# Three-pass gate chunk, tap sums on TensorE, a new order of work and warm-up matmuls in a convolution and two feed-forward layers

## The chip, the cores and the metric

The kernel runs on one core of one Trainium2 chip. The metric is the device time of one execution, in microseconds (us). Its parts are TensorE (PE, with PEld for its weight loads), VectorE (DVE), ScalarE (ACT), GpSimd (POOL) and SyncE (SP), which here only issues DMAs.

## The reference

Batch 2, sequence 4160, model width 192, 8 heads, 7 taps, inner width 1024, all in float32 for the reader (the weights come to the chip as 64-bit words and are narrowed there).

```python
def _attn_ref(x, weight_gen):          # 7-tap dynamic convolution
    w = softmax over the 7 taps of weight_gen      # (B, S, 8, 7)
    return einsum('bshk,bskhg->bshg', w, windows of 7 rows of x)

def _moe_ref(x, mu_k, mu_r, w_k, w_v, w_r):
    xk = mu_k * x + (1.0 - mu_k) * x_prev          # x_prev: x shifted by one row
    xr = mu_r * x + (1.0 - mu_r) * x_prev
    k = np.maximum(xk @ w_k, 0.0)                  # 192 -> 1024
    v = k * k @ w_v                                # 1024 -> 192
    r = 1.0 / (1.0 + np.exp(-(xr @ w_r)))          # the gate, 192 -> 192
    return r * v

def _moe2_ref(x, w_in, conv_w, w_out):
    h = np.maximum(x @ w_in, 0.0)                  # 192 -> 1024
    conv_out = 3-tap convolution of h along the sequence, by column
    return h * sigmoid(conv_out) @ w_out           # 1024 -> 192
```

The output is `_moe2_ref(_moe_ref(_attn_ref(x)))`.

## The kernel before, in words

**Tiles.** The sequence is cut into ten tiles (`SIZES`: 238, 238, seven of 476, 352), each with two batches. The inner width is cut into eight chunks of 128 (`fi` or `j`). A value in float32 is kept as a high and a low part in a matmul type of fewer bits, so that one product of two such values takes three matmul passes.

**Attention** (`attention`, 530). For each slot of a tile `token` (538) makes the seven products of rows and softmax weights in one instruction over 1344 elements (`prod`), then sums them over the taps. For tile 0 the products are made on DVE and the sum is seven matmuls with the identity on PE (`total`). For every later tile POOL makes the product and three adds. Two `rows` buffers and two `prod` buffers go round.

**Mixing** (`mixing`, 574). The sums are transposed on PE, mixed with the row before (`mu`, `onemu`) and split: `xA` holds model columns 0 to 127 (high and low), `xB` packs the last 64 columns, high part on one half of the lanes and low part on the other; SP copies these halves from `rm` and a scratch buffer.

**First layer.** `gate_r` (664) makes the gate for 128 output columns, `k=0`, and for the other 64, `k=1`; the columns of `k=1` are kept twice, so both halves of the lanes hold them. `passes_in` (660) is five passes: two weights parts by the high part of `xA`, one by the low part, two by `xB`. `moe1` (682) makes the chunk, relu, square, split (`s`), and `out_passes` (797) five passes into the banks `am` and `ar`. `mix_out` (818) multiplies by the gate and writes `X = x2[b]`: rows 0 and 1 high and low of columns 0 to 127, rows 2 and 3 the last 64.

**Second layer.** `moe2` (854) makes a chunk in bank `pc` (five passes), relu, three taps, sigmoid, product, the high part `g` by ACT (`c7`) and the low part by DVE, or by POOL from tile 7 on (`c8`); `out_passes` into `bm` and `br`; `store` (913) sends it out.

**Weights.** Sixteen chunks are fetched in the first part of the run (`prepare`, 478). `narrow` (399) turns a chunk of 64-bit words into float32 with ACT, DVE and two PE matmuls (identity and `signs`), and `split` (423) takes high and low part with one more PE matmul of `signs`.

**Order.** Nothing is issued directly. Every piece of work is put on a plan with `at(t, ...)` at a due time; the table `ORDER` shifts single entries of that plan by number (368). `Program.schedule` then walks through all recorded operations with a cost for each (`cost`), takes for each engine the ready operation that is due first, and replays the result engine by engine. That is why nearly all instructions carry line 237 in the profile (650 in the changed kernel). SP works its DMAs off in that order, one after the other: an entry whose semaphores are not there holds back all behind it.

Of the kernel before, what the change touches and what calls it, by code (L numbers as in the profile page):

```python
# [96 lines left out]
class Program:
# [986 lines left out]
```

## Time and profile before

| | |
|---|---|
| runs of the kernel | 734.06, 736.1, 736.75 us; median 736.1 |
| profiled execution, its own time | 739.15 us |
| profiled execution, span | 737.3 us |
| instructions | 10455 |
| PE busy | 706.5 us (96%), 3475 instructions |
| ACT / DVE / POOL busy | 646.6 (88%) / 580.1 (79%) / 537.8 us (73%) |
| mean granted TensorE clock | 0.989 of full speed |
| chain that ended last | PE 80%, POOL 8%, ACT 6%, issue 3%, DVE 2%, DMA 1% |

The span reaches from the first to the last instruction; the profiled execution's own time is 1.85 us more, and lies 3.05 us above the median. A PE record lasts longer than the pace at which PE goes on, since matmuls overlap at their ends: starts of successive records show the pace.

### The profile page before, as it was taken

The page shows a single profiled execution, that of the slowest core. Times are in us where ns is not written, and L with a number is a line of the kernel's source. Part 1 is how long each engine was busy: PE and PEld are TensorE (multiplying, and loading weights), DVE is VectorE, ACT ScalarE, POOL GpSimd, SP SyncE. Part 2 cuts the span into 40 slices and gives each one's busy share as a digit, 9 for nine tenths or more (in the row PEclk, how much of TensorE's full clock was granted, in tenths as well). Part 3 has the DMA queues.
Part 4 walks back from the last instruction along what each step waited for, and adds up shares of the span by engine and source line. Part 5 has one row for each costly group of instructions (what it writes and reads, how often), then busy time and mean ns, then how long its engine had stood idle before and what let it go on. Part 6 is the DMA issues. An engine that isn't in the chain of part 4 may idle for free.

```text
span 737.3 us, 10455 instructions
## 1 busy us (share of the span) xinstructions
PE 706.5 (96%) x3475; PEld 607.1 (82%) x3475; DVE 580.1 (79%) x959; ACT 646.6 (88%) x1340; POOL 537.8 (73%) x392
## 2 busy tenths in 40 slices
PE   4899988999999999999999999999999999999996
PEld 4687966888778888888888888888888888899995
DVE  5865968887998988787878787978796758686775
ACT  2788859999989999899989898989899989899986
POOL 1998997898999899999999999999022323242333
PEclk9899999999999999999999999999999999999999
DMA  8667112101211320231112202210002000200000
GB/s 271 196 198 228 56 54 54 39 35 59 68 39 55 88 75 1 73 80 48 54 58 57 87 1 69 74 48 1 21 15 59 1 20 7 55 0 21 1 21 29
DMA packets 18149, 44.58 MB, mean 60 GB/s; under 512 B 2864, under 2 KB 13616, under 8 KB 17968
## 3 DMA queue, kind: packets, MB, share of 16 engines
q1 hardware_dynamic: 18096, 43.93, 19.7%
q8 instruction: 27, 0.44, 0.3%
q14 instruction: 26, 0.21, 0.1%
HBM read 27.40 MB, written 6.39 MB: 46 GB/s over the span
## 4 chain that ended last, share of the span: by engine, by line
PE 80%; POOL 8%; ACT 6%; issue 3%; DVE 2%; DMA 1%; POOLq 0%; SPq 0%; ACTq 0%; DVEq 0%
PE pa L237 25%; PE pc L237 18%; PE bm L237 12%; PE am L237 11%; PE br L237 8%; PE ar L237 7%; POOL prod L237 5%; ACT pa L237 1%; DMA mu<-in_mu_dram 1%; ACT pc L237 1%; POOL s L237 1%; ACT L237 1%; DVE stage L237 1%; POOL xA L237 1%; POOL tok L237 0%
## 5 line engine op out<-in xcount | busy, mean ns | idle before, releaser
L237 DVE SCALAR_TENSOR_TENSOR pc<-h,cw,pc 128x476 f32<-128x476 f32 (+1 forms) x276 | 194.3, 705 | 40.4 <-ACT pc L237 37.4
L237 POOL TENSOR_TENSOR prod<-rows,sw 128x1344 f32<-128x1344 f32 x68 | 210.4, 3096 | 16.1 <-PE pa L237 15.2
L237 ACT ACTIVATE pa<-pa 128x476 f32<-128x476 f32 (+2 forms) x284 | 153.1, 540 | 31.7 <-PE pa L237 28.5
L237 POOL TENSOR_TENSOR prod<-prod 128x576 f32<-128x576 f32 (+1 forms) x132 | 161.5, 1223 | 9.3
L237 PE MATMUL bm<-g,wo 128*128 128x476 f32 (+1 forms) x411 | 133.1, 378 | 3.3 <-ACT g L237 2.8
L237 PE MATMUL am<-s,wv 128*128 128x476 f32 (+2 forms) x464 | 135.1, 359 | 0.0
L237 PE MATMUL pa<-xA,wkA 128*128 128x476 f32 (+2 forms) x450 | 117.6, 366 | 2.0 <-DVE s L237 1.5
L237 POOL TENSOR_TENSOR g<-stage,g 128x476 fp32r<-128x476 f32 (+1 forms) x41 | 47.5, 1158 | 97.5 <-ACT g L237 93.6
L237 PE MATMUL pc<-x,wiA 128*128 128x478 f32 (+1 forms) x414 | 113.2, 379 | 0.7 <-ACT x L237 0.6
L237 PE MATMUL ar<-s,wv 128*128 128x476 f32 (+2 forms) x336 | 106.5, 355 | 3.6 <-ACT s L237 3.6
L237 DVE TENSOR_TENSOR s<-pa,s 128x476 fp32r<-128x476 f32 (+1 forms) x139 | 88.1, 634 | 18.7 <-ACT s L237 18.2
L237 PE MATMUL br<-g,wo 128*128 128x476 f32 (+1 forms) x274 | 102.5, 375 | 0.0
L237 PEld LDWEIGHTS pa<-xA,wkA 128*128 128x128 f32 x450 | 79.7, 189 | 19.1 <-DVE s L237 5.5
L237 ACT ACTIVATE pc<-h,cw 128x476 f32<-128x476 f32 (+1 forms) x138 | 92.4, 670 | 1.2
L237 PEld LDWEIGHTS am<-s,wv 128*128 128x128 f32 x464 | 82.1, 189 | 11.2 <-ACT s L237 0.9
L237 DVE TENSOR_TENSOR pc<-h,pc 128x476 f32<-128x476 f32 x96 | 62.8, 654 | 33.7 <-ACT pc L237 33.5
L237 PEld LDWEIGHTS bm<-g,wo 128*128 128x128 f32 x411 | 75.9, 188 | 15.4 <-ACT g L237 4.3
L237 ACT ACTIVATE pc<-pc 128x476 f32<-128x476 f32 (+1 forms) x148 | 81.2, 548 | 8.2 <-DVE pc L237 6.5
L237 PEld LDWEIGHTS pc<-x,wiA 128*128 128x128 f32 x414 | 76.2, 190 | 12.7 <-DVE g L237 2.0
L237 ACT ACTIVATE h<-pc 128x478 f32<-128x478 f32 (+1 forms) x138 | 79.0, 573 | 8.4 <-PE pc L237 7.5
L237 PE MATMUL pa<-xB,wkB 128*128 128x476 f32 (+2 forms) x300 | 84.5, 361 | 0.6 <-DMA xB<-mk 0.6
L237 PE MATMUL pc<-x,wiB 128*128 128x478 f32 (+1 forms) x276 | 82.4, 377 | 0.0
(161 smaller groups left out, 1190.0 us busy)
## 6 DMA issues: line engine op xcount, KB each, us to landing
rows<-in_x_dram SPq DMA_DIRECT2D x14, 960.0 KB, 4.8
xB<-rm SPq DMA_DIRECT2D x28, 119.0 KB, 2.3
rows<-in_x_dram SPq DMA_DIRECT2D x4, 768.0 KB, 6.5
xB<-mk SPq DMA_DIRECT2D x16, 119.0 KB, 2.3
rows<-in_x_dram SPq DMA_DIRECT2D x2, 864.0 KB, 4.3
out_dram<-stage SPq DMA_DIRECT2D x7, 238.0 KB, 2.0
out_dram<-om SPq DMA_DIRECT2D x7, 238.0 KB, 2.0
stage<-in_moe_w_v_dram SPq DMA_DIRECT2D x4, 384.0 KB, 6.0
```

The source lines that it names most:

```text
L237: getattr(self.real[eng], method)(*a, **k)
```

## The change

- `gate_r`, `k=1`: the weights of the 64 columns are now stored as [high | low] side by side in 128 columns (`swap`, two DMAs), so that three passes give high and low products at once; `fold` copies the upper 64 lanes down with ACT and adds them with DVE, the sigmoid runs on 64 lanes, and a DMA copies the result to the other 64 lanes. This holds for tiles 2 to 9.
- `mix_out`: the ACT copy of 64 lanes into `X[0:64, 3]` becomes a DMA from `X[0:64, 2]`.
- `SUMS`: six slots of tiles 1 and 2 have their taps summed by seven matmuls on PE and an ACT copy, not by POOL.
- `MODES`: seven of the sixteen weight chunks are narrowed and split without PE, with two more DVE operations.
- `softmax`: for the later tiles the addition of 1e-9 goes from DVE to ACT (seven instructions).
- Last tile, last batch: the high part of chunks 0 to 4 goes from ACT to POOL (`HIGH`), the low part of chunks 6 and 7 from POOL to DVE (`LOWS`), and the last `out_passes` ends `ar`'s bank ahead of `am`'s (`back`).
- `WARM`: 18 matmuls of `signs` over 256 columns into the idle bank `ar`, ahead of PE's first instruction.
- `mu` comes with the first softmax load; its own DMA is gone. The last softmax load is due later (20.5, hold 60).
- The table `ORDER` is replaced as a whole.

The diff, without the table and without the layout on the host:

```diff
+WARM = 18
+HIGH = range(5)
+LOWS = {(NTILE - 1, NB - 1, k) for k in range(6, NF)}
+SUMS = {(1, 1, 0), (1, 1, 1), (2, 0, 2), (2, 0, 3), (2, 1, 2), (2, 1, 3)}
+MODES = [0, 0, 0, 0, 0, 0, 0, 0, 2, 2, 2, 0, 2, 2, 2, 2, 2]
...
         if method == "dma_start":
-            return 0.45, 0.0
+            return 0.58 if src == ["SBUF"] else 0.45, 0.0
...
             eng, method, a, k = self.ops[i][:4]
+            if eng == "PE" and self.warm:
+                self.warm = self.warm()
             getattr(self.real[eng], method)(*a, **k)
...
         def s5():
-            DVE.tensor_scalar(z, z, 1e-9, None, op0=ALU.add)
+            if bank is None:
+                ACT.activation(z, z, ACTF.Copy, bias=1e-9)
+            else:
+                DVE.tensor_scalar(z, z, 1e-9, None, op0=ALU.add)
             DVE.reciprocal(m, z)
...
     def split(dst_hi, dst_lo, x):
+        if isinstance(x, Parts):
+            px, zl, zr = x.aps
+            ACT.copy(dst_hi, px)
...
+                DVE.tensor_tensor(zl, px, f(dst_hi), op=ALU.subtract)
+                DVE.tensor_tensor(dst_lo, zr, f(zl), op=ALU.add)
+            return
...
-            if i < 1:
+            if i < 1 or (i, b, l) in SUMS:
...
                     for k in range(KS):
                         PE.matmul(z, lhsT=ident, rhs=y[:, k], start=(k == 0), stop=(k == KS - 1))
                     x = tok_t[i][:, :, b * DM:b * DM + DM]
+                    if i:
+                        ACT.copy(x[:, l], z)
+                        return
...
-            sl = slice(128 * k, 128 * k + 128)
-            mm(p[:, :N], passes_in(wrA, wrB, xin[i, b, 1, 0], xin[i, b, 1, 1], sl, N))
+            A, B = xin[i, b, 1, 0], xin[i, b, 1, 1]
+            if k:
+                mm(p[:, :N], [(wrA[:, 0, 128:256], A[:, 0, :N]), (wrA[:, 0, 128:256], A[:, 1, :N]), (wrB[:, 0, 128:256], B[:, :N])])
+            else:
+                mm(p[:, :N], passes_in(wrA, wrB, A, B, slice(0, 128), N))
+
+        def fold():
+            a = attt_r()[0:64, :N]
+            ACT.copy(a, st["p"][64:128, :N])
+            DVE.tensor_tensor(st["p"][0:64, :N], st["p"][0:64, :N], a, op=ALU.add)
 
         def sg():
             r = r_r[k]()
             r_t[k] = r
-            ACT.activation(r[:, :N], st["p"][:, :N], ACTF.Sigmoid)
-
+            ACT.activation(r[h, :N], st["p"][h, :N], ACTF.Sigmoid)
+            if k:
+                SP.dma_start(out=r[64:128, :N], in_=r[0:64, :N])
...
         def a1():
-            ACT.copy(X[0:64, 3, c], r[0:64, :N])
             ACT.copy(X[:, 2, c], r[:, :N])
+            SP.dma_start(out=f(X[0:64, 3, c]), in_=f(X[0:64, 2, c]))
...
-            ACT.copy(g[:, 0, :N], st["q"][:, :N])
+            if (i, b) == (NTILE - 1, NB - 1) and fi in HIGH:
+                POOL.tensor_copy(g[:, 0, :N], st["q"][:, :N])
+            else:
+                ACT.copy(g[:, 0, :N], st["q"][:, :N])
 
         def c8():
             g = st["g"]
-            (POOL if i >= ALONE else DVE).tensor_tensor(g[:, 1, :N], st["q"][:, :N], f(g[:, 0, :N]), op=ALU.subtract)
+            (POOL if i >= ALONE and (i, b, fi) not in LOWS else DVE).tensor_tensor(g[:, 1, :N], st["q"][:, :N], f(g[:, 0, :N]), op=ALU.subtract)
...
     def consts():
-        SP.dma_start(out=mu, in_=mus)
...
+    def swap():
+        for W in (wrA, wrB):
+            SP.dma_start(out=f(W[:, 0, DM:256]), in_=f(W[:, 1, 128:DM]))
+
+    at(30.5, swap)
...
+    def warm():
+        for _ in range(WARM):
+            nc.tensor.matmul(ar_r.tiles[0][:, 0:256], lhsT=signs[:, 0:128], rhs=signs[:, 0:256], start=True, stop=True)
+
+    prog.warm = warm
```

**Where the order moves.** In the rows below a name with a number is one buffer; what is in brackets are the semaphores an instruction waits for (of an engine, or of a DMA queue).

The first place is POOL's start, the tokens of tile 1 (`rows1` holds one batch, `rows0` the other). Before:

```order
L237 TENSOR_TENSOR prod1_84<-rows1_82,sw_112 128x1344 [waits DMAHW0_49,DMAHW6_49,DVE_49,PE_49]
L237 TENSOR_TENSOR prod0_83<-rows1_82,sw_112 128x1344 [waits PE_49]
L237 TENSOR_TENSOR prod1_84<-rows0_81,sw_112 128x1344 [waits DMAHW2_49,DVE_49,DMAHW7_49,PE_49,Pool_49]
L237 TENSOR_TENSOR prod0_83<-rows0_81,sw_112 128x1344 [waits PE_49,Pool_49]
L237 TENSOR_TENSOR prod0_83<-prod0_83 128x576 [waits Pool_49]
```

and in the changed kernel:

```order
L650 TENSOR_TENSOR prod0_82<-rows1_81,sw_111 128x1344 [waits DMAHW0_49,DMAHW6_49,DVE_49,PE_49]
L650 TENSOR_TENSOR prod1_83<-rows1_81,sw_111 128x1344 [waits DVE_49,PE_49]
L650 TENSOR_TENSOR prod0_82<-rows0_80,sw_111 128x1344 [waits DMAHW1_49,DVE_49,DMAHW5_49,PE_49,Pool_49]
L650 TENSOR_TENSOR prod0_82<-prod0_82 128x576 [waits Pool_49]
L650 TENSOR_TENSOR prod0_82<-prod0_82 128x384 [waits Pool_49]
```

POOL's first product now goes into the buffer of the first tap sum, `prod0`, where before it went into that of the second, `prod1`; and two products for PE's sums stand ahead of the first adds in both.

The second place is PE at the tap sums and transposes of tile 2, among the first layer of tile 1 and the second of the first unit. Before:

```order
L237 MATMUL pa1_114<-ident_64,tok0_85 128x128 [waits Pool_49]
L237 MATMUL pa1_114<-ident_64,tok0_85 128x128 x3
L237 MATMUL ar_118<-s0_105,wv_70 128x238 [waits Activation_49]
L237 MATMUL ar_118<-s0_105,wv_70 128x238 x2
L237 MATMUL ar_118<-s0_105,wv_70 128x238 [waits DVE_49]
L237 MATMUL ar_118<-s0_105,wv_70 128x238 x6
```

and in the changed kernel:

```order
L650 MATMUL pa1_113<-prod0_82,ident_63 128x192 [waits Pool_49]
L650 MATMUL pa1_113<-prod0_82,ident_63 128x192 x6
L650 MATMUL ar_117<-s1_105,wv_69 128x238 [waits DVE_49]
L650 MATMUL ar_117<-s1_105,wv_69 128x238 x5
L650 MATMUL pa1_113<-ident_63,tok0_84 128x128 [waits Activation_49]
L650 MATMUL pa1_113<-ident_63,tok0_84 128x128
L650 MATMUL pc1_115<-prod1_83,ident_63 128x192 [waits Pool_49]
L650 MATMUL pc1_115<-prod1_83,ident_63 128x192 x6
L650 MATMUL pa1_113<-ident_63,tok0_84 128x128 x2
L650 MATMUL pa0_112<-ident_63,tok0_84 128x128
```

The transposes (`tok0`) waited for POOL's last add; now they wait for ACT's copy of a sum that PE itself made from POOL's product.

The third place is SP's queue at the load of rows for the next tiles. Before:

```order
L237 DMA rows0_81<-in_x_dram 128x1920 [waits DMAHW7_49,Pool_49]
L237 DMA rows1_82<-in_x_dram 128x1920 [waits DMAHW0_49,Pool_49]
L237 DMA out_0_dram<-stage_76 128x476 [waits DMAHW1_49,Activation_49]
L237 DMA out_0_dram<-att0_87 64x476 [waits DMAHW2_49,DVE_49]
L237 DMA xB01_98<-rm00_91 64x476 [waits DMAHW3_49,PE_49,Activation_49]
```

and in the changed kernel:

```order
L650 DMA rows0_80<-in_x_dram 128x1920 [waits DMAHW7_49,Pool_49]
L650 DMA x2_1_74<-x2_1_74 64x476 [waits DMAHW0_49,PE_49,Activation_49]
L650 DMA rows1_81<-in_x_dram 128x1920 [waits DMAHW1_49,Pool_49]
L650 DMA r10_103<-r10_103 64x476 [waits DMAHW2_49,DVE_49,Activation_49]
L650 DMA out_0_dram<-stage_75 128x476 [waits DMAHW3_49,Activation_49]
L650 DMA out_0_dram<-stage_75 64x476 [waits DMAHW4_49,DVE_49]
L650 DMA x2_0_73<-x2_0_73 64x476 [waits DMAHW5_49,PE_49,Activation_49]
```

The copies of the gate (`r10`) and of `X` (`x2_1`, `x2_0`) stand in the same queue, some of them behind a load of rows that waits for POOL to leave its buffer.

## Rows read from the trace of the kernel before

**Rows 1.** Busy time of the engines in five stretches of the run.

```profile
core 0: us, PE busy (x) PEld busy (x) DVE busy (x) ACT busy (x) POOL busy (x), PEclk, DMA share, GB/s
0.00:20.00 20.00, 9.51 (x38) 8.09 (x38) 11.42 (x22) 5.84 (x15) 4.21 (x9) 1.00 0.79 259
20.00:85.00 65.00, 60.49 (x389) 51.41 (x390) 49.60 (x96) 54.51 (x143) 59.89 (x43) 0.95 0.61 189
85.00:125.00 40.00, 32.28 (x163) 26.42 (x163) 29.33 (x46) 28.87 (x56) 33.95 (x25) 0.91 0.18 50
...
250.00:500.00 250.00, 249.93 (x1168) 213.91 (x1167) 204.70 (x329) 228.02 (x456) 241.03 (x164) 1.00 0.19 57
720.00:737.30 17.30, 11.16 (x55) 8.57 (x55) 9.38 (x19) 10.65 (x25) 6.58 (x7) 0.92 0.10 31
```

**Rows 2.** The same view, two stretches of 2 us after tile 1.

```profile
92.00:94.00 2.00, 0.73 (x7) 0.53 (x5) 1.28 (x2) 2.00 (x5) 1.96 (x2) 1.00 0.00 0
98.00:100.00 2.00, 2.00 (x9) 1.80 (x8) 0.66 (x1) 0.81 (x3) 1.92 (x3) 0.55 0.00 0
```

**Rows 3.** Chain that ended last: start us, us, what; the same place of two tiles.

```profile
351.71 1.51 PE pa L237 x9
...
427.08 1.53 PE pa L237 x9
```

**Rows 4.** Timeline of PE at a gate chunk: start us, us, engine, line, operation.

```profile
215.77 0.60 PE L237 MATMUL pa<-xA,wrA 128*128 128x476 f32 x2
216.20 0.59 PE L237 MATMUL pa<-xB,wrB 128*128 128x476 f32 x2
```

**Rows 5.** Timeline of PE at tap sums: the first two, and a later one.

```profile
10.22 6.88 PE L237 MATMUL pa<-prod,ident 128*128 128x192 f32 x28 [10.22 <-DVE prod L237]
...
23.14 2.44 PE L237 MATMUL pa<-prod,ident 128*128 128x192 f32 x14
```

**Rows 6.** Timeline of PE at weight chunks: identity pairs and a `signs` matmul.

```profile
22.91 0.40 PE L237 MATMUL br<-wkA,signs 128*128 128x512 f32 x1
...
66.16 1.02 PE L237 MATMUL bm<-stage,ident 128*128 128x512 f32 x2
...
74.40 0.81 PE L237 MATMUL bm<-stage,ident 128*128 128x384 f32 x2
```

**Rows 7.** Timeline of POOL: first product, adds and next product, last add of tile 2.

```profile
16.54 6.04 POOL L237 TENSOR_TENSOR prod<-rows,sw 128x1344 f32<-128x1344 f32 x2 [15.19 <-PE pa L237]
...
83.12 2.53 POOL L237 TENSOR_TENSOR prod<-prod 128x576 f32<-128x576 f32 x2
...
86.28 3.08 POOL L237 TENSOR_TENSOR prod<-rows,sw 128x1344 f32<-128x1344 f32 x1
...
104.60 0.59 POOL L237 TENSOR_TENSOR tok<-prod 128x192 f32<-128x192 f32 x1
```

**Rows 8.** Timeline of ACT and of DVE in the first 10 us.

```profile
2.23 0.30 ACT L237 ACTIVATE signs<-ident 128x128 fp32r<-128x128 f32 x1
...
8.43 0.17 DVE L237 TENSOR_SCALAR onemu<-mu 128x4 f32<-128x4 f32 x1 [2.58 <-DMA mu<-in_mu_dram]
```

**Rows 9.** Timeline of POOL, DVE and PE, 215 to 220 us.

```profile
215.07 3.08 POOL L237 TENSOR_TENSOR prod<-rows,sw 128x1344 f32<-128x1344 f32 x1
...
216.14 2.06 DVE L237 TENSOR_SCALAR stage<-stage 128x48 f32<-128x48 f32 x1
...
219.43 0.93 PE L237 MATMUL pa<-xA,wkA 128*128 128x476 f32 x3 [1.35 <-DVE s L237]
```

**Rows 10.** Timeline of DVE at `mix_out`, an operation over 64 lanes.

```profile
202.58 0.65 DVE L237 TENSOR_TENSOR x<-ar,x 64x476 fp32r<-64x476 f32 x1
```

**Rows 11.** Timeline of POOL in the tail: the last low part.

```profile
731.31 0.94 POOL L237 TENSOR_TENSOR s<-stage,s 128x354 fp32r<-128x354 f32 x1 [0.67 <-ACT s L237]
```

**Rows 12.** Page, DMA issues: queue, count, KB each, us from issue to landing.

```profile
xB<-rm SPq DMA_DIRECT2D x28, 119.0 KB, 2.3
```

**Rows 13.** Waits of SP: waited for, us in total, times, longest us.

```profile
SPq L237 <- POOL prod L237: 199.4, 16, 27.2
```

More of the change, by code (lines that the diff above doesn't have):

```diff
@@ L103, in __init__ @@
         self.real = {"PE": nc.tensor, "ACT": nc.scalar, "DVE": nc.vector, "POOL": nc.gpsimd, "SP": nc.sync}
+    warm = None
     def engine(self, name):
@@ L251, in conv_moe_kernel @@
 @with_exitstack
-def conv_moe_kernel(ctx: ExitStack, tc: tile.TileContext, xp, wg_first, wg_rest, mus, w_k, w_v, w_r, w_in, conv_w, w_out, out):
+def conv_moe_kernel(ctx: ExitStack, tc: tile.TileContext, xp, wg_first, wg_rest, w_k, w_v, w_r, w_in, conv_w, w_out, out):
     nc = tc.nc
@@ L285, in __call__ @@
             return self.tiles[(self.n - 1) % len(self.tiles)]
-    mu = new("mu", [128, 4])
     onemu = new("onemu", [128, 4])
@@ L311, in conv_moe_kernel @@
     wz_r = Ring([t.rearrange("p a b -> p (a b)") for t in g_r.tiles[:2]])
+    wl_r = Ring([t.rearrange("p a b -> p (a b)") for t in g_r.tiles[2:]])
     rows_r = ring("rows", 2, [128, max(SLOTS) + PAD, DM])
@@ L328, in conv_moe_kernel @@
     KH = KS * NH
-    sw = new("sw", [128, sum(slots), KS, NH])
+    both = new("sw", [128, 4 + sum(slots) * KH])
+    mu = both[:, 0:4]
+    sw = both[:, 4:].rearrange("p (s k h) -> p s k h", k=KS, h=NH)
     sm = []
@@ L395, in fetch, with __init__, rearrange, __getitem__ @@
         return st
-    on_pe = [False]
+    mode = [0]
+    class Parts:
+        def __init__(self, *aps):
+            self.aps = aps
+        def rearrange(self, *a, **k):
+            return Parts(*(x.rearrange(*a, **k) for x in self.aps))
+        def __getitem__(self, c):
+            return Parts(*(x[c] for x in self.aps))
     def narrow(st, n):
@@ L404, in narrow @@
         x, y, z = px.bitcast(U32), py.bitcast(U32), wy_r()[:, :n]
-        if on_pe[0]:
+        ACT.activation(px, f(hi), ACTF.Prelu, scale=2.0 ** -112, alpha=-(2.0 ** 32))
+        if mode[0] == 0:
             zr = wz_r()[:, :n]
-            ACT.activation(px, f(hi), ACTF.Prelu, scale=2.0 ** -112, alpha=-(2.0 ** 32))
             DVE.tensor_scalar(z, x, 3, None, op0=ALU.logical_shift_left)
@@ L414, in narrow @@
             return px
-        ACT.activation(px, f(hi), ACTF.Copy, scale=2.0 ** -112)
         DVE.tensor_scalar(x, x, 3, None, op0=ALU.logical_shift_left)
-        DVE.scalar_tensor_tensor(out=x, in0=hi, scalar=0x80000000, in1=x, op0=ALU.bitwise_and, op1=ALU.bitwise_or)
         DVE.tensor_scalar(y, x, 0xFF800000, None, op0=ALU.bitwise_and)
-        DVE.scalar_tensor_tensor(out=f(z), in0=lo, scalar=2.0 ** -52, in1=py, op0=ALU.mult, op1=ALU.mult)
-        DVE.tensor_tensor(px, px, f(z), op=ALU.add)
-        return px
+        zr = wz_r()[:, :n] if mode[0] == 1 else py
+        DVE.scalar_tensor_tensor(out=zr, in0=lo, scalar=2.0 ** -52, in1=py, op0=ALU.mult, op1=ALU.mult)
+        return Parts(px, wl_r()[:, :n], zr)
     def split(dst_hi, dst_lo, x):
+        if isinstance(x, Parts):
+            px, zl, zr = x.aps
+            ACT.copy(dst_hi, px)
+            if mode[0] == 1:
+                DVE.tensor_tensor(zl, px, f(dst_hi), op=ALU.subtract)
+                PE.matmul(px, lhsT=signs[:, 0:128], rhs=zl, start=True, stop=False, skip_group_check=True)
+                PE.matmul(px, lhsT=signs[:, 0:128], rhs=zr, start=False, stop=True, skip_group_check=True)
+                ACT.copy(dst_lo, px)
+            else:
+                DVE.tensor_tensor(zl, px, f(dst_hi), op=ALU.subtract)
+                DVE.tensor_tensor(dst_lo, zr, f(zl), op=ALU.add)
+            return
         ACT.copy(dst_hi, x)
-        if on_pe[0] and prog.space(x) == "PSUM":
+        if prog.space(x) == "PSUM":
             PE.matmul(x, lhsT=signs[:, 128:256], rhs=dst_hi, start=False, stop=True, skip_group_check=True)
@@ L486, in use @@
             def use(st=st, n=n, go=go, j=j):
-                on_pe[0] = j < 16
+                mode[0] = MODES[j]
                 go(narrow(st[0], n))
@@ L495, in softmax_load @@
     def softmax_load(j, wg, t, hold=0.0):
-        w = sm[j][0]
-        at(t, lambda: SP.dma_start(out=w.rearrange("p s k h -> p (s k h)"), in_=wg), hold)
+        w = both[:, (4 + KH * soft_at[j]) * (j > 0):4 + KH * soft_at[j + 1]]
+        at(t, lambda: SP.dma_start(out=w, in_=wg), hold)
     def softmax(j, a, b, eng, times, bank):
@@ L676, in sg @@
             r_t[k] = r
-            ACT.activation(r[:, :N], st["p"][:, :N], ACTF.Sigmoid)
+            ACT.activation(r[h, :N], st["p"][h, :N], ACTF.Sigmoid)
+            if k:
+                SP.dma_start(out=r[64:128, :N], in_=r[0:64, :N])
+        h = slice(0, 64 if k else 128)
         at(t, go)
-        at(t + 0.3, sg)
+        if k:
+            at(t + 0.2, fold)
+        at(t + (0.6 if k else 0.3), sg)
     def moe1(i, b, fi, t):
@@ L795, in mix_out_half, with out_passes @@
         at(t + 0.4, d2)
-    def out_passes(W, fi, s, n, am, ar, one=False):
+    def out_passes(W, fi, s, n, am, ar, one=False, back=False):
         s0, s1 = s[:, 0, :n], s[:, 1, :n]
@@ L802, in out_passes @@
         PE.matmul(ar[:, :n], lhsT=W[:, fi, 2], rhs=s0, start=a and not one, stop=False, skip_group_check=one)
-        PE.matmul(am[:, :n], lhsT=W[:, fi, 0], rhs=s1, start=False, stop=z, skip_group_check=one)
-        PE.matmul(ar[:, :n], lhsT=W[:, fi, 2], rhs=s1, start=False, stop=z, skip_group_check=one)
+        for p, k in ((ar, 2), (am, 0)) if back else ((am, 0), (ar, 2)):
+            PE.matmul(p[:, :n], lhsT=W[:, fi, k], rhs=s1, start=False, stop=z, skip_group_check=one)
     def carry(i, b, t):
@@ L889, in c7 @@
             st["g"] = g
-            ACT.copy(g[:, 0, :N], st["q"][:, :N])
+            if (i, b) == (NTILE - 1, NB - 1) and fi in HIGH:
+                POOL.tensor_copy(g[:, 0, :N], st["q"][:, :N])
+            else:
+                ACT.copy(g[:, 0, :N], st["q"][:, :N])
         def c8():
             g = st["g"]
-            (POOL if i >= ALONE else DVE).tensor_tensor(g[:, 1, :N], st["q"][:, :N], f(g[:, 0, :N]), op=ALU.subtract)
+            (POOL if i >= ALONE and (i, b, fi) not in LOWS else DVE).tensor_tensor(g[:, 1, :N], st["q"][:, :N], f(g[:, 0, :N]), op=ALU.subtract)
         def go2():
@@ L899, in go2 @@
                 acc2["r"] = br_r()
-            out_passes(wo, fi, st["g"], N, acc2["m"], acc2["r"])
+            out_passes(wo, fi, st["g"], N, acc2["m"], acc2["r"], back=last and b == NB - 1 and fi == NF - 1)
         at(t + 0.5, go)
@@ L971, in conv_moe_kernel @@
     softmax(2, 0, slots[2], DVE, (0.9, 0.91, 0.92, 0.93, 0.94, 0.95), am_r.tiles[0])
-    softmax_load(3, wg_rest[:, (slots[1] + slots[2]) * KH:], 18.2, 50.0)
+    softmax_load(3, wg_rest[:, (slots[1] + slots[2]) * KH:], 20.5, 60.0)
     for j in range(NTILE - 3):
@@ L1018, in conv_moe_kernel @@
         fn()
+    def warm():
+        for _ in range(WARM):
+            nc.tensor.matmul(ar_r.tiles[0][:, 0:256], lhsT=signs[:, 0:128], rhs=signs[:, 0:256], start=True, stop=True)
+    prog.warm = warm
     with tc.manual_schedule():
         prog.schedule()
-_ARGS = ("x", "first", "rest", "mu", "moe_w_k", "moe_w_v", "moe_w_r", "moe2_w_in", "moe2_conv_w", "moe2_w_out")
+_ARGS = ("x", "first", "rest", "moe_w_k", "moe_w_v", "moe_w_r", "moe2_w_in", "moe2_conv_w", "moe2_w_out")
 def _layout(inputs):
@@ L1048, in _layout @@
     w = np.asarray(inputs["weight_gen"]).transpose(0, 1, 3, 2)
+    mu = np.stack([c for k in "kr" for m in [rows(inputs["moe_mu_" + k]).reshape(DM)]
+                   for c in (m[:128], np.concatenate([m[128:], m[128:]]))], axis=1)
     a = {
         "x": np.concatenate([np.zeros_like(x[:, :PAD]), x], axis=1),
-        "first": chunks(w, 0, 1),
+        "first": np.concatenate([mu, chunks(w, 0, 1)], axis=1),
         "rest": chunks(w, 1, NTILE),
-        "mu": np.stack([c for k in "kr" for m in [rows(inputs["moe_mu_" + k]).reshape(DM)]
-                        for c in (m[:128], np.concatenate([m[128:], m[128:]]))], axis=1),
         "moe_w_k": rows(inputs["moe_w_k"]),
```

502 rows, old and new, of the table ORDER are left out of this document.

## The prediction

> **What bounds the kernel now.** I read the busy times by stretch first, then the chain that ended last, then the timelines of the places that the change touches.
>
> By stretch [rows 1], PE has 0.07 us without work in 250 to 500 us. There the kernel is bound by PE's own work, at full clock, and the chain shows it tile by tile: the same nine gate and chunk passes come again after 427.08 - 351.71 = 75.37 us [rows 3]. ACT is next (228 of 250 us), and POOL's 241 are not in the way. In that middle only fewer PE instructions can help.
>
> Before 125 us it is otherwise. PE stands idle 4.5 us in 20 to 85 and 7.7 us in 85 to 125, and the granted clock there is 0.95 and 0.91 of full, so 65 x 0.05 = 3.3 and 40 x 0.09 = 3.6 us more are lost to half clock. The short stretches show the sequence: in 92 to 94 us PE is busy 0.73 of 2 us, and in 98 to 100 it is busy throughout with the clock at 0.55, that is mostly at 1.2 of 2.4 GHz [rows 2]. PE waits there for tile 2's attention: POOL starts its first product at 16.54, after a sum on PE, and works through token after token until 105.2 us [rows 7]. The first two tap sums also run slowly: 28 records took 6.88 us, where a later sum of 14 took 2.44 [rows 5]. Less the 0.17 us that a group's last record outlasts its pace (two passes start 216.20 - 215.77 = 0.43 us apart and last 0.60 [rows 4]), a sum is 2.27 us, and the two lost 6.71 - 4.54 = 2.2 us. In all 21.3 us are lost ahead of 125 us. In the last 17.3 us PE is idle for 6.1 us [rows 1].
>
> **The sum**, against the profiled execution, 739.15 us, which is 3.05 us above the median of the runs.
>
> 1. Gate. For `k=1` of tiles 2 to 9 and both batches two passes fall away: 14 x 2 passes of 476 columns and 2 x 2 of 352. A pass is 0.43 / 2 = 0.215 us [rows 4], one of 352 columns 0.160 by its width: 28 x 0.215 + 4 x 0.160 = **-6.7 us**, all of it in the stretch where PE has no idle time. In place of them come an ACT copy, a DVE addition (0.65 us for such an operation [rows 10]), a sigmoid and a copy by SP. They are hidden as long as the bank is free in time: ahead of the next writer of that bank PE has at least 14 passes to do in all sixteen cases, 14 x 0.215 = 3.0 us, and the copy, the addition and the sigmoid need about 3 x 0.65 = 2.0. Without that cover each would cost up to 2.0.
>
> 2. Start and first tiles. PE gets six more sums, 6 x 2.27 = +13.6 us. Of the seven chunks it loses, three are 512 wide: an identity pair (1.02 - 0.17 = 0.85) and two `signs` matmuls (0.40 - 0.17 = 0.23), 1.31 us each; four are 384 wide: 0.81 - 0.17 = 0.64 and two of 0.17 (three quarters of 0.23), 0.98 us each [rows 6]. That is -7.8. So PE's work in this stretch grows by 5.8 us, and the question is how much of the 21.3 lost it fills. POOL is relieved of six times three adds: from 83.12 to the next product at 86.28 is 3.16 us [rows 7], 19.0 in all. Its first product now reuses the buffer of the first sum, not the second: earlier by between 0 and 4 us, since the first sum at full pace could end at 10.22 + 2.27 = 12.5; I take 3. Then tile 2's attention ends at about 83 instead of 105 us, before PE runs out of other work. The two extra DVE operations of each of the seven chunks, some 0.65 each, come to 9 us on an engine busy 49.6 of 65. Ends: all 21.3 vanish, -21.3 + 5.8 = -15.5; none vanish, +5.8. I take 8 of the 21.3 as remaining, nearer the good end, because POOL's relief is larger than PE's idle time: -13.3 + 5.8 = **-7.5**.
>
> The warm-ups belong here. They need `signs`, there at 2.53 us [rows 8]. 256 columns at the pace of [rows 4] are 0.116 us, at half clock 0.23, so 18 of them take at most 4.2 us and end by 6.7 us, and PE's first sum waits for DVE's product until about 10. PE is idle for about 3 us between. If the clock has fallen again by then, or never rose, 2.2 us of the loss stays.
>
> 3. `mu`: its DMA ended the wait for `onemu` at 8.43 us [rows 8]; the first product follows at once. Rows for that product must land too, so the gain is small: **-0.3** (0 to -0.6).
>
> 4. Additions of 1e-9 on ACT. At 216.14 such an instruction of 48 columns took 2.06 us on DVE; it ended with POOL's product (215.07 + 3.08), and PE then stood 1.35 us for DVE [rows 9]. This wait goes: **-1.4** (0 to -1.4). Late next is ACT, which has 22 us of slack in 250.
>
> 5. Tail. The last low part took 0.94 us on POOL [rows 11]; over 64 lanes of 476 columns DVE takes 0.65 [rows 10], 0.48 for 354 by width. Two of them on the path: -0.9. ACT loses five copies and PE's last bank is read earlier; I take **-2** in all (0 to -3 of the 6.1 idle).
>
> The Trainium skill ("SBUF — State Buffer", section "Who interferes with whom") says that a DVE instruction with two SBUF inputs contends with a GpSimd instruction that reads SBUF. That speaks against the low parts on DVE: each could wait out one POOL operation, the tail's term would be about -0.2 instead of -2. The DVE row at 216.14 agrees with the rule's neighbour for other forms, but no row shows a two-input DVE operation beside POOL in the tail.
>
> 6. New waits. 33 more DMAs stand in SP's queue, each 2.3 us from issue to landing by the nearest row [rows 12]. Sixteen gate copies have most of a half tile to land, sixteen of `X` serve the fifth pass of a chunk. I take **+1.5** (0 to +8, half a us per tile and batch).
>
> Sum: -6.7 - 7.5 - 0.3 - 1.4 - 2 + 1.5 = -16.4. For the profiled execution that is 722.8, and for the median **720 us**.
>
> **Rivals.**
>
> A. The clock does not hold at the start. Then the 2.2 us of the cold sums stay, and the 3.3 of half clock in 20 to 85, where weights and tiles still come in bursts: 720 + 5.5 = 725 us. For it: the idle 3 us after the warm-ups, and the half clock after 92 to 94 us [rows 2]. Against: more PE work (5.8 us) in the same stretch. The Trainium skill ("TensorE: Matmul & The Clock Gate", section "Why this matters for your kernels") advises against idle gaps between bursts of matmuls, as they bring the low clock back; the trace agrees in [rows 2], where 1.2 GHz follows a stretch with PE busy 0.73 of 2 us. By that rule the warm-ups do nothing and this rival is the likely course of the first 20 us.
>
> B. The first tiles are not bound by POOL but by the chains through ACT and DVE (relu, square, split), so that of the 21.3 us nothing beyond PE's added work is won back: item 2 is 0 and not -7.5, and if the additional work isn't hidden either, +5.8. Then -16.4 + 13.3 = -3.1, 733 us. For it: ACT is busy 2.00 of 2 us at 92 to 94 us, when PE idles [rows 2]. Against: POOL is busy 59.9 of the 65 us [rows 1] and is through with tile 2's attention only at 105.2 [rows 7].
>
> C. SP's queue, on the other side. The copies of gate and `X` stand behind loads of rows that wait for POOL; such waits were 16 and up to 27.2 us long [rows 13]. A late gate copy holds up `mix_out`, and with it the banks `ar` and `am` and all PE work behind them. If each of the 16 tile and batch pairs waits for one landing of 2.3 us, that is +36.8, and 720 + 36.8 = 757. It decides from (16.4 + 3.7) / 16 = 1.26 us per pair. Against: the order puts the loads where POOL is due to be through, and PE's queue holds a dozen passes of other work at most places.
>
> **How the numbers follow.** A measurement can tell about 0.5% from no change, 3.7 us. The forecast has 0.62, A 0.20, B 0.12, C 0.06. The forecast's own range takes 4 to 13 of the 21.3 as remaining and the new waits from 0 to +4: 714 to 728. The range to hold 8 in 10 goes down to where all 21.3 us vanish (item 2 at -15.5, 712), with the tail's better end and hardly a new wait 710, and up over A and B with a small part of the waits, 735. C lies outside. Faster: forecast and A, 0.82; within 0.5%: B, 0.12; slower: C, 0.06.
>
> **What would show it.** Right: 74.5 us per tile in the chain in place of 75.37 (four passes fewer a tile); POOL done with tile 2's attention near 83 us; PE idle under 6 us in 20 to 125; no `TENSOR_SCALAR` of 2 us on DVE beside a POOL product. The first sums at 2.3 us each show the warm-ups working, at 3.3 each not. Wrong: PE waiting for DMAs of `r` or `X` in the middle; PE idle in 250 to 500 for a gate's fold; ACT or DVE ending PE's waits near 90 us as before.

## The result and the profile after

The changed kernel takes 714.2 us (median of 4 runs, 713.0 to 714.6), the kernel before in the same runs 736.15 us. The ratio is 0.970, 95% interval 0.968 to 0.973: 21.9 us faster. The forecast was 16.4 us less, 720 us.

The traced execution has a span of 712.3 us against 737.3, 25.0 us less. Of these about 3 us are no gain: the traced execution of before was among its slowest (E9). The busy times by stretch, with the columns of [rows 1]:

```profile
0.00:20.00 20.00, 16.16 (x72) 14.34 (x73) 14.70 (x31) 8.98 (x22) 6.80 (x9) 1.00 0.74 259
20.00:85.00 65.00, 61.75 (x437) 56.03 (x437) 59.26 (x118) 54.65 (x138) 59.85 (x39) 1.00 0.63 190
85.00:125.00 40.00, 39.46 (x217) 34.55 (x216) 33.06 (x55) 36.58 (x75) 37.88 (x27) 1.00 0.18 51
125.00:250.00 125.00, 125.00 (x583) 106.09 (x583) 110.40 (x181) 119.50 (x241) 115.72 (x80) 1.00 0.26 74
250.00:500.00 250.00, 250.00 (x1173) 214.05 (x1172) 210.08 (x341) 229.34 (x461) 232.20 (x160) 1.00 0.18 54
```

In 20 to 125 us PE is idle 3.3 + 0.5 = 3.8 us where it was 12.2, and the granted clock is 1.00 where it was 0.95 and 0.91 [rows 1]. From 125 to 500 us PE has no idle time at all. For 125 to 250 the kernel before had this row:

```profile
125.00:250.00 125.00, 123.13 (x573) 103.54 (x572) 111.31 (x181) 115.90 (x229) 115.30 (x80) 1.00 0.16 49
```

so another 1.9 us of idle time are gone there. POOL's last products for tile 2 end at 78.83 + 6.08 = 84.9 us, near the 83 that the prediction names:

```profile
78.83 6.08 POOL L650 TENSOR_TENSOR prod<-rows,sw 128x1344 f32<-128x1344 f32 x2
```

PE's timeline shows tile 2's sums:

```profile
78.44 2.44 PE L650 MATMUL pc<-prod,ident 128*128 128x192 f32 x14
...
82.69 2.44 PE L650 MATMUL pa<-prod,ident 128*128 128x192 f32 x14
...
85.86 2.44 PE L650 MATMUL pc<-prod,ident 128*128 128x192 f32 x14
88.14 0.49 PE L650 MATMUL pa<-ident,tok 128*128 128x128 f32 x3
```

Each row of 14 records is one sum (seven matmuls, two records each), three of tile 2's four; the last ends at 88 us and the transposes follow at once, where POOL's last add ended at 105.2 [rows 7]. The gate's second chunk, in PE's timeline of one tile:

```profile
610.31 0.60 PE L650 MATMUL pa<-xA,wrA 128*128 128x476 f32 x2
610.74 0.38 PE L650 MATMUL pa<-xB,wrB 128*128 128x476 f32 x1
```

are the three passes in place of five [rows 4]. What it cost in DMAs stands on the page, in the columns of [rows 12]:

```profile
r<-r SPq DMA_DIRECT2D x14, 119.0 KB, 2.2
x<-x SPq DMA_DIRECT2D x14, 119.0 KB, 2.2
```

They land in 2.2 us and PE does not wait for them: from 125 to 700 us its list of waits (waited for, us in total, times, longest us) has one row, for POOL.

```profile
PE bm L650 <- POOL s L650: 0.2, 1, 0.2
```

### The profile page after: what moved, and what is told of

The parts are those of the page before. It is cut to its first block, busy times and chain, and to the rows that moved or that the text cites. A ratio compares the mean times of both kernels' runs of the same rounds, so it can differ in the third digit from the quotient of the medians.

```text
span 712.3 us, 10592 instructions
## 1 busy us (share of the span) xinstructions
PE 699.3 (98%) x3513; PEld 607.8 (85%) x3513; DVE 587.0 (82%) x992; ACT 637.1 (89%) x1337; POOL 519.8 (73%) x377
## 4 chain that ended last, share of the span: by engine, by line
PE 87%; DVE 5%; ACT 3%; DMA 2%; issue 1%; POOL 1%; SPq 0%; DVEq 0%; POOLq 0%; ACTq 0%
PE pa L650 26%; PE pc L650 21%; PE bm L650 12%; PE am L650 12%; PE br L650 8%; PE ar L650 8%; DMA stage<-in_moe_w_out_dram 1%; DVE stage L650 1%; DVE pc L650 1%; ACT pc L650 1%; DVE am L650 1%; ACT pa L650 1%; POOL prod L650 0%; DVE s L650 0%; ACT h L650 0%
## 5 line engine op out<-in xcount | busy, mean ns | idle before, releaser
L650 DVE SCALAR_TENSOR_TENSOR pc<-h,cw,pc 128x476 f32<-128x476 f32 (+1 forms) x270 | 190.4, 707 | 29.7 <-ACT pc L650 26.8
L650 ACT ACTIVATE pa<-pa 128x476 f32<-128x476 f32 (+2 forms) x290 | 156.9, 547 | 9.9 <-PE pa L650 8.1
L650 POOL TENSOR_TENSOR prod<-prod 128x576 f32<-128x576 f32 x120 | 147.0, 1225 | 8.2
L650 PE MATMUL bm<-g,wo 128*128 128x476 f32 (+1 forms) x411 | 135.7, 377 | 0.6 <-POOL g L650 0.6
L650 DVE TENSOR_TENSOR s<-pa,s 128x476 fp32r<-128x476 f32 (+1 forms) x142 | 90.1, 634 | 26.3 <-ACT s L650 25.8
L650 PEld LDWEIGHTS pa<-xA,wkA 128*128 128x128 f32 x468 | 81.7, 188 | 15.1 <-DVE s L650 2.9
L650 ACT ACTIVATE pc<-h,cw 128x476 f32<-128x476 f32 (+1 forms) x135 | 90.6, 671 | 1.0
L650 ACT ACTIVATE h<-pc 128x478 f32<-128x478 f32 (+1 forms) x135 | 77.7, 576 | 10.6 <-PE pc L650 10.3
L650 PEld LDWEIGHTS pc<-x,wiA 128*128 128x128 f32 x414 | 74.0, 188 | 14.7 <-DVE g L650 3.6
L650 ACT ACTIVATE pc<-pc 128x476 f32<-128x476 f32 (+1 forms) x142 | 78.4, 552 | 7.7 <-DVE pc L650 7.1
L650 ACT CAST s<-pa 128x476 fp32r<-128x476 f32 (+1 forms) x142 | 79.5, 561 | 1.2 <-PE ar L650 0.4
```

Of the source, the lines that this page charges most:

```text
L650: getattr(self.real[eng], method)(*a, **k)
```

## The experiments

Runs that share a chip are E1 to E4, E5 to E8 and E9 to E12; times of different groups are compared by their ratios to the kernel before on the same chip, one hundredth of a ratio being 7.4 us. E1 is the changed kernel itself.

**E1, the base.**

> The changed kernel once more, as the base for the runs beside it on the same chip. Every theory: 714 us within 1 us, a ratio of 0.970 to the kernel before.

Measured: 714.7 us, ratio 0.972 (0.969 to 0.974).

**E2, no warm-ups.**

```diff
-WARM = 18
+WARM = 0
```

> The changed kernel without the 18 warm-up matmuls, everything else in the same order. Theory (the warm-ups do nothing, because the first two tap sums took 6.64 us with them and 6.88 without, and PE's pace rises only within these sums in both): 714 us within 0.7 us, the first two sums still 6.5 to 6.9 us. Rival (they lift part of the low clock at the start): 2 us slower, 716, and the first two sums over 7.5 us or half clock somewhere in 20 to 125 us.

Measured: 716.3 us, ratio 0.973 (0.971 to 0.976); the difference to E1, 1.3 us by the ratios, is within the intervals. PE's timeline, of E2 and then of E1:

```profile
7.67 7.56 PE L650 MATMUL pa<-prod,ident 128*128 128x192 f32 x28 [7.67 <-DVE prod L650]
```

```profile
2.59 4.21 PE L1482 MATMUL ar<-signs 128*128 128x256 f32 x18 [2.59 <-ACT signs L650]
7.78 6.44 PE L650 MATMUL pa<-prod,ident 128*128 128x192 f32 x28 [0.98 <-DVE prod L650]
```

The first two sums are 1.1 us longer without warm-ups than in E1, as the rival said, so the theory that they do nothing falls for the sums; for the time it can't be told.

**E8, 22 warm-ups.**

```diff
-WARM = 18
+WARM = 22
```

> The changed kernel with 22 warm-up matmuls, so that they end where the first tap sum starts (7.7 us) and the gap of 0.95 us is gone. Theory (the gap let the low clock stand on): the first two sums take under 5.5 us where they took 6.4 to 6.6, 1 to 2 us faster, 713. Rival (when the pace rises differs from execution to execution, and the gap has no part in it): 714 to 715, the first two sums anywhere from 4.8 to 6.6 us.

Measured: 716.1 us, ratio 0.974 (0.971 to 0.977), not faster than E1. The first two sums ran at the pace of later ones (two of 2.27 us [rows 5] and the overhang of 0.17 are 4.71):

```profile
2.58 4.50 PE L1482 MATMUL ar<-signs 128*128 128x256 f32 x22 [2.58 <-ACT signs L650]
7.64 4.79 PE L650 MATMUL pa<-prod,ident 128*128 128x192 f32 x28 [0.56 <-DVE prod L650]
```

But 18 warm-ups gave 4.79 us as well, in E3, E6, E7, E11 and E12, and 6.4 to 6.6 in E1 and the first trace: with gaps of 0.56 to 1.38 us between warm-ups and sums the pace differs from execution to execution, and the length of the gap doesn't decide it. In E4's trace the gap was 2.99 us; there the two sums took 6.42 us, and the granted clock behind the gap was half:

```profile
10.00:12.00 2.00, 2.00 (x8) 2.00 (x7) 2.00 (x4) 0.82 (x2) 0.00 (x0) 0.50 0.99 393
```

In all other traces that column reads 1.00 throughout the first 20 us, whether the sums run fast or slowly; that their slow pace there is a low clock is not shown by it. Nor does the earlier end help much: in 20 to 85 us PE is idle 4.65 us in E8 and 3.25 in the changed kernel's first trace, so a good part of what was won at the start is idle time later. PE's two longest waits in that stretch of E8 are not for weights: before one of tile 2's sums PE waits for DVE's `s`, and before a gate chunk for its input `xA`. The others, of at most 0.6 us each, are mostly for weights.

```profile
PE pc L650 <- DVE s L650: 1.2, 1, 1.2
PE pa L650 <- ACT xA L650: 0.9, 1, 0.9
```

The chain that ended last in the changed kernel (start, us, what) passes in that stretch through the load of a weight chunk, so the weights have a part in it without being the whole:

```profile
39.91 9.02 DMA stage<-in_moe_w_out_dram
48.95 2.01 DMA wiB<-x
```

**E3, the gate in five passes.** `gate_r` calls `passes_in` for both chunks, with the fold, the copy of `r` and `swap` left out.

```diff
-            if k:
-                mm(p[:, :N], [(wrA[:, 0, 128:256], A[:, 0, :N]), (wrA[:, 0, 128:256], A[:, 1, :N]), (wrB[:, 0, 128:256], B[:, :N])])
-            else:
-                mm(p[:, :N], passes_in(wrA, wrB, A, B, slice(0, 128), N))
+            mm(p[:, :N], passes_in(wrA, wrB, A, B, slice(128 * k, 128 * k + 128), N))
...
-                SP.dma_start(out=r[64:128, :N], in_=r[0:64, :N])
```

> The changed kernel with the gate's second chunk in five passes on 128 lanes again, so without the fold, the copy of the gate by DMA and the rearranged weights. Theory (32 passes on a path without idle time, and the fold hidden): 6.7 us slower, 721. Rival (the fold and the copies cost PE waits that eat up part of it): slower by under 4 us. Second rival (the table of offsets no longer fits and PE gets new waits): slower by over 9 us, with PE idle in 125 to 700 us.

Measured: 723.2 us (720.8 to 728.8), ratio 0.983 (0.980 to 0.986): 8.5 us slower by the medians, 5.9 by the spans of the traced executions (719.0 and 713.1). PE is busy 5.4 us more over the span, 705.0 against 699.6 us in E1, and idle 0.9 us in 125 to 250 us, where E1 has none, so a small part may be the new order. The term of 6.7 us lies within what these runs can tell, and the fold and the copies cost nothing that can be seen.

**E4, the sums on POOL.**

```diff
-SUMS = {(1, 1, 0), (1, 1, 1), (2, 0, 2), (2, 0, 3), (2, 1, 2), (2, 1, 3)}
+SUMS = set()
```

> The changed kernel with all tap sums of tiles 1 and 2 on POOL again. Theory (the first 125 us are bound by POOL's tokens): PE loses 13.6 us of work and POOL gets 19 us more of it; tile 2's attention ends 15 us later or more, PE is idle 15 to 20 us in 20 to 125 instead of 3.8 and the clock falls to half there at least once: 8 us slower, 722 (718 to 728). Rival (ACT and DVE chains are the bound, POOL isn't): PE's shorter work shows, 714 or up to 10 us faster.

Measured: 725.0 us, ratio 0.985 (0.983 to 0.988), 10.3 us slower though PE has 13.6 us less to do (the prediction's six sums of 2.27). By stretch:

```profile
20.00:85.00 65.00, 56.23 (x388) 49.82 (x386) 58.67 (x120) 53.72 (x136) 57.64 (x42) 0.95 0.60 175
85.00:125.00 40.00, 31.36 (x153) 26.07 (x154) 29.26 (x49) 29.64 (x58) 34.95 (x25) 0.91 0.22 70
```

Idle are 8.8 + 8.6 = 17.4 us, the clock is again 0.95 and 0.91 as in the kernel before, and tile 2's last add on POOL ends late:

```profile
105.36 0.60 POOL L650 TENSOR_TENSOR tok<-prod 128x192 f32<-128x192 f32 x1
```

The edit leaves the due times of the plan as they are, and the other engines' work nearly so: over the span DVE is busy 588.0 us against 587.3 in E1, ACT 636.2 against 637.2, POOL 538.0 against 519.6. So the loss comes from POOL's longer work, or from how the planner sorts anew around it; these two are not parted. PE itself does not wait for POOL there. Its two longest waits, 8.5 us together between 83 and 98 us, end with ACT's `g`, of the second layer of the tiles ahead:

```profile
PE bm L650 <- ACT g L650: 8.5, 2, 4.9
```

In the kernel before, too, the longest waits of 85 to 125 us end with ACT, where the prediction says that PE waits for tile 2's attention:

```profile
PE ar L237 <- ACT s L237: 3.4, 2, 2.0
PE bm L237 <- ACT g L237: 2.4, 3, 0.9
```

What is missing is other work. PE's first chunk of tile 2 (476 columns), in E4 and then in the changed kernel:

```profile
110.11 0.70 PE L650 MATMUL pa<-xA,wkA 128*128 128x476 f32 x2
```

```profile
95.88 0.70 PE L650 MATMUL pa<-xA,wkA 128*128 128x476 f32 x2
```

It comes 14 us later. That PE would have gone on with tile 2 in place of waiting for ACT is argued from these rows, no wait shows it. The traced execution, 727.45 us, is the slowest of four (the others 724.5 to 725.0): its rows came late at the start,

```profile
7.77 3.03 DVE L650 TENSOR_TENSOR prod<-rows,sw 128x1344 f32<-128x1344 f32 x2 [1.80 <-DMA rows<-in_x_dram]
```

and about 2 us of what the trace is longer are no price of the edit.

**E6, all chunks narrowed through PE.**

```diff
-MODES = [0, 0, 0, 0, 0, 0, 0, 0, 2, 2, 2, 0, 2, 2, 2, 2, 2]
+MODES = [0] * 16 + [2]
```

> The changed kernel with all weight chunks narrowed through PE matmuls again. Theory (with the tap sums on PE the first 125 us are bound by PE, which has 3.8 us idle there): PE gets 7.8 us more and the time rises by 5 to 8 us, 721. Rival (the DVE operations were the dearer form, DVE is busy 59.3 of 65 us there): DVE loses 9 us and the time changes by under 2 us.

Measured: 724.9 us, ratio 0.988 (0.984 to 0.991): 11.7 us slower by the ratios than E1, more than the theory's 5 to 8 and more than the 7.8 us of matmuls. PE has new idle time behind the stretch:

```profile
85.00:125.00 40.00, 37.64 (x219) 33.52 (x220) 29.02 (x48) 32.70 (x67) 38.54 (x27) 1.00 0.25 76
125.00:250.00 125.00, 122.26 (x568) 102.96 (x567) 108.55 (x178) 117.94 (x236) 113.46 (x80) 1.00 0.21 61
```

2.4 + 2.7 us, where the changed kernel has 0.5 and 0. So the planner, with offsets that fit other work, also made a worse order; the edit's own price and that of the order can't be parted here.

**E7, the old table with all edits.** `ORDER` is that of before; the new entries `fold` and `swap` take the offset of the entry ahead and do not count.

> The changed kernel with the old table of offsets (the entries that are new take the offset of the entry ahead of them). Theory (the edits carry the gain, but the first 125 us depend on what is ahead in each queue): 721 to 728, PE idle 8 to 15 us in 20 to 125, and under 1 us in 250 to 500. Rival (the edits carry all of it): 714 to 717. Second rival (the table carries it): 730 or more.

Measured: 730.95 us, ratio 0.993 (0.992 to 0.995): 5.0 us faster than before, 15.9 slower than E1 by the ratios. By its time the second rival came nearest; the theory's time is missed, though its idle times hold (14.2 us in 20 to 125, none in 250 to 500). By stretch:

```profile
20.00:85.00 65.00, 58.97 (x403) 51.96 (x401) 56.48 (x114) 50.55 (x130) 51.59 (x36) 0.97 0.60 184
85.00:125.00 40.00, 31.83 (x162) 27.67 (x163) 24.72 (x40) 31.15 (x57) 35.09 (x24) 0.88 0.18 51
125.00:250.00 125.00, 125.00 (x588) 106.74 (x587) 110.54 (x181) 117.02 (x236) 118.38 (x82) 1.00 0.20 62
```

PE is idle 6.0 + 8.2 us and at half clock for part of the rest. One of tile 2's sums shows both: it waits for its product on POOL, and takes 4.22 us in place of 2.44.

```profile
87.72 4.22 PE L246 MATMUL pa<-prod,ident 128*128 128x192 f32 x14 [1.79 <-POOL prod L246]
```

From 125 to 690 us there is no idle time with the old table either. What the table is worth lies nearly all ahead of that. And this run shows the gate's price by tile, since its order repeats from tile to tile as that of the kernel before does: the same nine passes come again in its chain after 460.21 - 385.88 = 74.33 us, where it was 75.37 [rows 3].

```profile
385.88 1.52 PE pa L246 x9
460.21 1.52 PE pa L246 x9
```

That is 1.0 us a tile for four passes, where 0.86 was priced.

**E10, the new table alone.** All edits undone but `mu`'s place and the due time of the last softmax load.

> The changed kernel with all edits undone but the new table, mu's place and the due time of the last softmax load: five gate passes, no tap sums of tiles 1 and 2 on PE, all chunks narrowed on PE, no warm-ups, the copies on ACT, the additions on DVE, the tail as before. Theory (table and edits only work together): 733 to 742, PE idle 15 us or more and the clock at half at least once in 20 to 125 us. Rival (the table alone carries most): 718 to 728, PE idle under 8 us in 20 to 125.

Measured: 738.1 us, ratio 1.0025 (1.0012 to 1.0039), 1.8 us slower than before.

```profile
85.00:125.00 40.00, 28.96 (x129) 23.80 (x128) 26.96 (x41) 26.66 (x50) 35.92 (x25) 0.83 0.21 68
```

PE is idle 11.0 us in this stretch, at a clock of 0.83, and 14.3 us in 20 to 125, just under the theory's 15. So edits alone bring -5.0, the table alone +1.8, both together -21: they can't be priced apart, and E7's second rival (the table carries the gain) falls.

**E5, only `mu` moved, in the kernel before.**

```diff
-    mu = new("mu", [128, 4])
...
+    both = new("sw", [128, 4 + sum(slots) * KH])
+    mu = both[:, 0:4]
...
-        SP.dma_start(out=mu, in_=mus)
```

> The kernel before with mu in the first softmax load and nothing else changed. Theory (mu's DMA held back the rows and with them everything at the start; in the changed kernel the first product starts at 6.05 us, before at 8.51): first product at 6 us, all of the start 2.4 us earlier, 2 to 2.5 us faster, 733.9. Rival (the prediction's term: the rows bound it anyway): 0.3 us, no difference that can be measured, the first product after 8 us.

Measured: 735.9 us against 736.3, ratio 1.0003 (0.999 to 1.0015): no difference. Yet the first product starts at 5.99 us in its trace, and its whole timeline lies 3 us ahead of that of before. The rival's number is right. Its reason, that the rows bind the product anyway, does not hold in this trace (in E4's it does, where they held it back until 7.77); E9 shows another. In 85 to 125 us the clock fell here as in the first trace of before:

```profile
85.00:125.00 40.00, 32.80 (x157) 26.80 (x157) 28.85 (x46) 29.20 (x57) 34.11 (x25) 0.91 0.17 50
```

**E9, the kernel before once more**, unchanged.

> The kernel before once more, with a trace of another execution. Theory (the traced execution of before, 739.15 us, was the slowest of all, and its excess lay at the start, where the DMA of mu came late; in most executions it doesn't): a span of 732 to 735 us, the first product at 6 to 6.5 us and the rest of the first 125 us as in the first trace, only 2 to 3 us earlier. Rival (mu always costs that): first product after 8 us, and the shorter span comes from the clock or from later.

Measured: 736.6 us; the traced execution took 733.8, span 732.1. DVE's timeline and three stretches:

```profile
5.84 0.16 DVE L237 TENSOR_SCALAR onemu<-mu 128x4 f32<-128x4 f32 x1
5.96 3.02 DVE L237 TENSOR_TENSOR prod<-rows,sw 128x1344 f32<-128x1344 f32 x2
```

```profile
20.00:85.00 65.00, 61.08 (x397) 51.62 (x396) 50.41 (x94) 55.14 (x142) 59.72 (x45) 0.95 0.62 189
85.00:125.00 40.00, 32.27 (x170) 26.29 (x171) 31.54 (x51) 31.80 (x63) 35.60 (x25) 1.00 0.18 50
125.00:250.00 125.00, 123.07 (x570) 103.12 (x568) 110.64 (x179) 115.72 (x227) 115.98 (x82) 1.00 0.18 54
```

In this execution `mu` came in time (3.7 us from issue to landing, 6.8 in the first trace), the product started at 5.96 and not at 8.51,

```profile
8.51 3.03 DVE L237 TENSOR_TENSOR prod<-rows,sw 128x1344 f32<-128x1344 f32 x2
```

and the clock didn't fall in 85 to 125 us though PE was idle there for the same 7.7 us. The idle times are the same in both traces and belong to the kernel. The late `mu` is in one of these two traces. The second loss of clock is the more frequent case: E5's trace has it too, and of the 49 executions of the kernel before that ran beside the experiments 16 had a mean clock of 0.993, like this one (733.6 to 735.8 us), the other 33 had 0.988 to 0.991 (735.2 to 738.1).

**E11, the tail undone.**

```diff
-HIGH = range(5)
-LOWS = {(NTILE - 1, NB - 1, k) for k in range(6, NF)}
+HIGH = ()
+LOWS = set()
...
-            out_passes(wo, fi, st["g"], N, acc2["m"], acc2["r"], back=last and b == NB - 1 and fi == NF - 1)
+            out_passes(wo, fi, st["g"], N, acc2["m"], acc2["r"], back=False)
```

> The changed kernel with the last tile's high parts on ACT and low parts on POOL, and the banks ended in the old order. Theory (the tail's term of the prediction, measured at about 0.9 us by PE's idle time in the last 25 us, 6.1 before and 5.3 after): 0.5 to 2 us slower, 716. Rival (the low parts on DVE wait for POOL and bring nothing): no change or 0.5 us faster.

Measured: 716.7 us, ratio 0.974 (0.972 to 0.976), 1.6 us slower than E1 by the ratios, within the intervals. In the last 25 us of the span PE is busy 18.61 us here, 18.86 in the kernel before and 19.73 in the changed kernel, about 1 us more. (The rest of this trace's longer span lies mostly in 20 to 85 us, which the edit does not touch: 5.1 us idle there against 3.25.)

```profile
690.70:715.70 25.00, 18.61 (x102) 15.88 (x100) 16.65 (x33) 18.04 (x44) 9.36 (x10) 1.00 0.09 26
```

```profile
687.30:712.30 25.00, 19.73 (x112) 17.51 (x110) 18.84 (x38) 18.28 (x42) 10.83 (x14) 0.98 0.09 26
```

**E12, the additions on DVE.**

```diff
-            if bank is None:
-                ACT.activation(z, z, ACTF.Copy, bias=1e-9)
-            else:
-                DVE.tensor_scalar(z, z, 1e-9, None, op0=ALU.add)
+            DVE.tensor_scalar(z, z, 1e-9, None, op0=ALU.add)
```

> The changed kernel with the seven additions of 1e-9 on DVE again; the planner orders the work around them anew. Theory (they stand behind POOL's products on DVE, and PE waits): 1 to 3 us slower, 717, with at least one such instruction over 1 us on DVE and PE idle over 1 us in 125 to 250. Rival (PE has other work meanwhile): 714 to 715, PE idle under 0.3 us in 125 to 250.

Measured: 717.0 us (715.7 to 719.9), ratio 0.975 (0.973 to 0.977), 2.4 us slower than E1 by the ratios, at the edge of what these runs can tell. One of the additions took long, as before [rows 9]:

```profile
174.04 2.00 DVE L650 TENSOR_SCALAR stage<-stage 128x64 f32<-128x64 f32 x1
```

PE is idle 0.64 us in 125 to 250 us, neither over 1 nor under 0.3. But this is not a wait for the long addition: 0.54 of it ends at 168.87 with ACT's `r`, and PE is busy throughout while the addition runs and after it.

```profile
174.00:180.00 6.00, 6.00 (x30) 5.13 (x29) 5.87 (x9) 5.18 (x12) 5.76 (x5) 1.00 0.09 23
```

So the long addition comes back, the wait behind it doesn't; where the 2.4 us come from, if they are more than noise, stays open, since the planner ordered some of the work anew.

The copy of `X` by DMA and the late due time of the last softmax load were not undone by themselves.

## Why the prediction was right, and where its sizes were off

The time lies in the range and moved the way that was forecast, by 21.9 us where 16.4 were forecast. By the steps of the sum:

1. **Gate, -6.7: right.** Three passes stand where five stood, E3 gives 5.9 to 8.7 us, and PE waits neither for a fold nor for a copy. The sign of 74.5 us per tile is met in E7, with 74.33; in the changed kernel no place recurs at a fixed distance. By E7 the term is a little small: 1.0 in place of 0.86 us a tile is about 1.1 us more over tiles 2 to 9 (an estimate).
2. **First tiles, -7.5: right direction, too small, the cause shown in part.** Of the 21.3 us lost before, 8 were taken as remaining. What remains in the first trace of the changed kernel is 3.8 us idle, nothing at half clock in 20 to 125, and 6.64 - 0.17 - 4.54 = 1.9 us in the slow first two sums, 5.7 in all: -21.3 + 5.8 + 5.7 = -9.8. (In E9's execution the loss of before was 3.9 + 7.7 + 3.3 + 2.3 = 17.2 us and not 21.3; but 33 of 49 executions of before had a mean clock of 0.988 to 0.991, like the first trace, and E9's had 0.993.) That POOL's work was the bound rests on E4, where giving the six sums back to POOL costs 10 us while PE and ACT have less to do; the waits themselves end with ACT, and the new order is not parted from it. What the step left out is the order: with the old table (E7) the same edits bring 5.0 us in all, less than the gate's term alone. The relief of POOL became time only with the order that puts other work at hand for PE, and that was not priced.
3. **`mu`, -0.3: right**, by E5 (0.4 us by the medians, none by the ratios). The trace of before showed a price of 2.5 us for it (first product at 8.51, in E9 at 5.96); as its 3.05 us above the median were subtracted as a whole, this did no harm.
4. **Additions, -1.4:** the idle time of 125 to 250 us fell by 1.9, and E12 is 2.4 us slower, with an interval of about that size. The direction is the same, but E12's long addition is followed by no wait of PE, so that the idle time went because of this edit is not shown.
5. **Tail, -2: too large.** PE's idle time in the last 25 us fell from 6.1 to 5.3, -0.9; E11 says 1.6 within wide bounds. The two low parts on DVE took 1.17 us together, where POOL takes 1.85 for them in E11 (from 708.68 on): 0.7 less, where 0.9 was priced. They ran when POOL was done (its last ended at 705.32, they began at 705.85), so the rule of the Trainium skill ("SBUF — State Buffer", section "Who interferes with whom") on two SBUF inputs beside GpSimd had no occasion here:

```profile
704.37 0.95 POOL L650 TENSOR_TENSOR s<-stage,s 128x354 fp32r<-128x354 f32 x1
```

```profile
705.85 1.17 DVE L650 TENSOR_TENSOR s<-stage,s 128x354 fp32r<-128x354 f32 x2
```

6. **New waits, +1.5: none.** No wait of PE for `r` or `X` copies is in the trace, so rival C had no ground.

With these sizes the sum is -6.7 - 9.8 - 0.3 - 1.9 - 0.9 = -19.6 us. For the 2.3 us up to the 21.9 measured there are only estimates: the gate's 1.1 above, and after each idle gap a record's 0.17 us of overlap [rows 4] is lost and counted as busy, and PE's records have about 40 gaps in the trace of before and 22 in that of the changed kernel, 18 x 0.17 = 3.1 us at most. No run parts these from the rest. Against E9's execution, whose loss was 17.2, the same working gives -15.2 (without the term of `mu`) where the spans differ by 19.8; there 4.6 us stay without a run that shows them.

Rival A was half right. The warm-ups do quicken the first two sums in most traced executions: 4.79 us in six of nine, 6.4 to 6.6 in three, without warm-ups 6.46 to 7.56. The gap behind them was 0.95 us in the changed kernel's first trace and not the 3 that were reckoned with, since the product came earlier; where it was 2.99, in E4, the clock fell. But whether the sums are quick makes no difference in the time that these runs could tell (E2, E8). The rest of rival A, half clock in 20 to 85 us, did not come. That PE had work there goes with this: in 20 to 125 us the changed kernel's first trace has 3.8 us of idle time and a clock of 1.00, E4, E7 and E10 have 14.2 to 17.4 us and lower clocks. That it is the whole cause is not shown: E9 held 1.00 in 85 to 125 us with 7.7 us idle in that stretch.

Rival B's time, 733 us, is far from what came. Its sign, ACT ending PE's waits near 90 us, is there whenever tile 2 is late (E4, as in the kernel before): the chains through ACT and DVE are what PE then waits on. But the changed kernel has the same chains, and with six sums fewer on POOL PE's waits in 85 to 125 us are down to 0.5 us.
